# Attention feeding a softplus network: chunks of 512 tokens throughout, a larger token ring, and weight work moved between engines

## The chip, the cores and the metric

The kernel runs on one core of one Trainium2 chip. The metric is device time in microseconds (us) of one execution; lower is better. Five engines work side by side, each on its own queue in order: TensorE (PE in the profile, with its weight loads as PEld), VectorE (DVE), ScalarE (ACT), GpSimd (POOL) and SyncE (SP), which here only starts transfers. They wait for each other by semaphores.

## What is computed

```python
# q, k, v: (8, 8, 576, 64), q and k large, so that the softmax is sharp
scores = q @ k.transpose(0, 1, 3, 2) / sqrt(64)
local   = (rel >= 0) & (rel < 32)                  # heads 0..3, rel = row - column
strided = (rel >= 0) & (same position modulo 32)   # heads 4..7
attn = softmax(where(mask, scores, -1e9))
x = (attn @ v).transpose(0, 2, 1, 3).reshape(4608, 512)
h = x @ w_in                                       # 512 x 2048
g = max(h, 0) + log1p(exp(-abs(h)))                # softplus
out = g @ w_out                                    # 2048 x 512
```

The network's weights arrive as float64, 8 bytes each, and are turned into float32 on the chip. Because the products must be more exact than one pass of TensorE in its fast 32-bit format, every operand of the network is kept as a high part and a low part (value minus high part), and each product is made of three: high by high, high by low weight, low by high weight.

## The kernel before, in words

**Attention.** Work goes by pairs of heads: 8 batches of 4 pairs, n = 0 to 31. A pair's steps are: load queries (`load_q`), keys (`load_k`) and values (`load_v`); lay the queries out (`lay_out_q`, lines 252 and 254); the scores of nine chunks of 64 keys in two parts (`scores`, line 315); the softmax on VectorE and ScalarE (lines 334 to 405); transposing the probabilities, in the first batch on TensorE with copies back (`early_transposes`, `early_copy`, lines 430 to 451), later on VectorE (`prob_transposes`, line 415); the weighted sums (`weighted`, line 466); and writing the result as high part (ScalarE, line 491) and low part (VectorE, line 489) into the token buffers (`x_part`). These buffers hold 1152 tokens, two batches, as a ring.

**Weights.** Both matrices are cut into 16 tiles of 128 x 512, 32 in all. Each is rebuilt from the two 32-bit halves of its float64 values: magnitude (`w_abs`, ScalarE, line 516), shift (`w_shift`, VectorE, line 520), sign (`w_sign`, VectorE, line 526), the last three bits from the lower half (`w_last`, VectorE, line 532), then the high part (`w_high`, ScalarE, line 538) and the low part (`w_low`, VectorE or GpSimd, line 542).

**Network.** Tokens go through it in chunks: 512, 256, and then ten of 384. A step is one chunk by one of 16 slices of 128 hidden units: the hidden product (`hidden`, line 556, 12 matmuls as wide as the chunk, tile `ph`), the softplus (`log_part` on ScalarE, lines 568 to 573, `softplus` on VectorE, line 577), its high and low part (`g_high`, `g_low`, lines 585 to 592), and the output product two steps later (`output`, line 599, 3 matmuls of 512 columns for each 128 tokens, tile `py`, one accumulator bank for each 128 tokens). At a chunk's end the banks are copied out and stored (`result`, lines 610 and 612).

**Order.** The first stage, attention of batches 0 and 1, all weight work, chunk 0 and the beginning of chunk 1, is written out by hand as a list of names, `FIRST`. A letter names the step and the number its pair or tile: q, k, v loads; D query layout; S scores; X, Y, x, E, Z, r, R, M softmax; T and C or P transposes; V weighted sums; H and L high and low token parts; wi and wo weight loads; a, B, c, d, h, l (with i or o) the six weight steps; F hidden; A, Ae, Al, u softplus; Gh, Gl parts; O output; Q... the same for chunk 1; y results. `ON_POOL` and `ON_VECTOR` name those that run on another engine than usual. Each engine gets its operations in the order of this list.

After that, `Plan` (a list scheduler with costs and due times written in the kernel) orders steps and pairs. The pairs of batches 2 to 7 are put between steps by `BATCH_AT`: four steps apart, batches 2 and 3 in chunks 2 and 3, 4 and 5 in chunks 5 and 6, 6 and 7 in chunks 8 and 9. Where another pair follows four steps later, its scores and the weighted sums of the pair before are one visit of TensorE (`joint`); the first pair of each group of eight has its scores alone, the last its sums alone. Four hidden steps of chunk 1 (`AHEAD`) belong to the written list.

**Buffers.** Laid-out queries, keys, transposed probabilities and values have two buffers each; accumulator memory has two banks for `ph`, four for `py`, one each for scores (`ps`) and sums (`po`). From batch 2 on the second part of the scores uses the fourth `py` bank, which chunks of 384 leave free.

Of the kernel before, what the change touches and what calls it, by code (L numbers as in the profile page):

```python
# [11 lines left out]
BF16 = mybir.dt.bfloat16  # L12
U32 = mybir.dt.uint32
# [22 lines left out]
q0 mask D01 W k0 D00 q1 D10 S00 D11 X00 Y00 S01 X01 x01 k1 wo5 q2 E00 Z00 S11 X11 S10 E01 r0 q3 R0  # L36
M0 k2 ao5 T01 D21 D20 D30 Bo5 co5 Y11 C01 do5 T00 C00 X10 x10 S20 X20 D31 T02 wi5 ai5 Bi5 E11 Z11
E10 ci5 S21 X21 di5 v0 V00 H00 C02 Y20 E20 k3 r1 x21 wi11 R1 M1 S31 L00 wi1 X31 v1 S30 Z20 V01
ai11 Bi11 E21 H01 T10 C10 wi2 ci11 di11 r2 x31 R2 T11 T12 L01 C11 V10 v2 ai1 X30 M2 wi0 Y30 T21
C12 ho5 lo5 hi5 wi3 li5 hi11 li11 H10 L10 v3 E30 Z30 E31 C21 r3 R3 T20 k5 C20 V11 H11 T22 Bi1 L11  # L40
# [12 lines left out]
X70 x70 hi13 hi12 li12 Gh8 Gl8 ho8 lo8 V51 u9 Gh9 Gl9 F10 A10 Ae10 P6 F12 v6 ai15 Bi15 H51 L51 O8
li13 Al10 u10 V60 F13 ao10 Bo10 co10 ai14 ao11 Bo11 E70 do10 ho10 Bi14 ci14 O9 di14 v7 ci15 di15
Gh10 Gl10 A12 Ae12 lo10 Al12 u12 S71 hi15 H60 A13 hi14 L60 ao12 co11 V61 H61 do11 li14 O10 L61
li15 X71 x71 E71 Bo12 co12 Gh12 Gl12 r7 R7 ho11 lo11 Ae13 M7 Al13 wo13 ao13 u13 Gh13 F14 Bo13 do12
O11 q8 D8 co13 do13 ho12 lo12 Gl13 F15 O12 ho13 lo13 P7 V70 A14 Ae14 ao14 Bo14 co14 O13 do14 A15
Ae15 Al14 u14 ao15 Bo15 H70 L70 V71 ho14 Qa0 Gh14 Gl14 lo14 O14 k9 co15 H71 do15 ho15 L71 Q0 q9
Al15 u15 QA0 Gh15 lo15 Gl15 Qu0 Qh0 Q2 O15 y0 y1 Ql0 QA2 Q1 Qu2 Qh2 Ob15 y3 QO0 QA1 Qu1 Q3 D9 k8
Qh1 Ql1 Ql2 QA3 Qu3 Qh3 v9 v8 y2 Ql3 QO1  # L60
# [9 lines left out]
ON_SCALAR = """  # L70

# [47 lines left out]
def attention_softplus_ffn(  # L119
# [21 lines left out]
    RING = 2 * S  # L141

    CH = [512, 256] + [384] * ((NT - 768) // 384)
# [7 lines left out]
    v_pool = ctx.enter_context(tc.tile_pool(name="v", bufs=2))  # L151
# [11 lines left out]

    qT_early, kT_early = (
        {
            n: x_pool.tile([P, RING], F32, tag=f"x{part}{PAIRS[n]}", name=f"early_{part}{n}")
            for n in (2, 3)
        }
        for part in "hl"
# [30 lines left out]
    nc.vector.memset(pt[0], 0.0)  # L200
    nc.gpsimd.memset(pt[1], 0.0)
# [3 lines left out]
    vs, pss, sts, pos = ({} for _ in range(4))  # L205
# [57 lines left out]
    def load_v(n):  # L263
        b, pair = order[n]
        if n < NPAIR:

            t = room[n]
        else:
            t = v_pool.tile([P, 2 * NTILE * D], F32, tag="v_in", name=f"v_{b}_{pair}")
# [13 lines left out]
    for n in range(NPAIR):  # L283
        zeros(n)
# [632 lines left out]
```

## Time and profile before

| | |
|---|---|
| median of 3 runs | 926.68 us (926.28 to 927.91) |
| the profiled execution: time | 927.21 us |
| its span, first to last instruction | 925.4 us |
| its granted TensorE clock, mean | 0.995 |
| TensorE busy | 908.2 us, 98% |
| VectorE busy | 622.5 us, 67% |
| ScalarE busy | 483.1 us, 52% |
| GpSimd busy | 63.0 us, 7% |
| read from and written to HBM | 47.91 MB and 9.44 MB |

The profile is of one execution. A page has the engines' busy time, then the span in 40 slices (a digit is the busy share in tenths; PEclk is the share of the clock that TensorE was granted). Other views of the same trace are used below: *windows* give each engine's busy time in stretches of the span; *groups* put instructions of one line, engine and tile together, with their count, busy time, mean length in ns, and the idle time before them with what ended it; the *chain of waits* goes back from the last instruction, at each step to what released it, and lists pieces with start and length; the *timeline* lists instructions in order. Matmuls are pipelined: their recorded lengths overlap, so the cost of one is the distance to the next start and not its length.

### The profile page before, as it was taken

The page shows a single profiled execution, that of the slowest core. Times are in us where ns is not written, and L with a number is a line of the kernel's source. Part 1 is how long each engine was busy: PE and PEld are TensorE (multiplying, and loading weights), DVE is VectorE, ACT ScalarE, POOL GpSimd, SP SyncE. Part 2 cuts the span into 40 slices and gives each one's busy share as a digit, 9 for nine tenths or more (in the row PEclk, how much of TensorE's full clock was granted, in tenths as well). Part 3 has the DMA queues.
Part 4 walks back from the last instruction along what each step waited for, and adds up shares of the span by engine and source line. Part 5 has one row for each costly group of instructions (what it writes and reads, how often), then busy time and mean ns, then how long its engine had stood idle before and what let it go on. Part 6 is the DMA issues. An engine that isn't in the chain of part 4 may idle for free.

```text
span 925.4 us, 16092 instructions
## 1 busy us (share of the span) xinstructions
PE 908.2 (98%) x6276; PEld 799.5 (86%) x6276; DVE 622.5 (67%) x1438; ACT 483.1 (52%) x935; POOL 63.0 (7%) x96
## 2 busy tenths in 40 slices
PE   7898999999999999999999999999999999999998
PEld 5586778998898888988899988989988898999997
DVE  8998995488878853367788873338888785433332
ACT  7887875455555544335555445335555543333433
POOL 4433530000000000000000000000000000000000
PEclk9998999999999999999999999999999999999999
DMA  9962302021122110002222111002112200000000
GB/s 332 324 234 94 104 26 92 1 79 43 55 78 72 44 30 35 1 14 89 58 57 77 45 54 51 1 1 89 43 43 64 69 17 1 35 1 1 35 1 34
DMA packets 49947, 58.37 MB, mean 63 GB/s; under 512 B 3152, under 2 KB 35024, under 8 KB 49872
## 3 DMA queue, kind: packets, MB, share of 16 engines
q1 hardware_dynamic: 49872, 57.36, 19.2%
q8 instruction: 49, 0.80, 0.4%
q14 instruction: 26, 0.21, 0.1%
HBM read 47.91 MB, written 9.44 MB: 62 GB/s over the span
## 4 chain that ended last, share of the span: by engine, by line
PE 88%; DVE 7%; ACT 2%; issue 2%; DMA 1%; POOL 1%; SPq 0%; DVEq 0%; POOLq 0%
PE py L599 42%; PE ph L556 40%; PE po L466 3%; PE ps L315 2%; DVE pt L415 2%; PE py L315 1%; DVE a_i L526 1%; DVE a_i L532 1%; DVE u L577 1%; DVE a_i L520 1%; DMA raw_q<-in_qk_dram 1%; DVE a_o L526 0%; DMA prob<-in_qk_dram 0%; ACT prob L357 0%; DVE a_o L532 0%
## 5 line engine op out<-in xcount | busy, mean ns | idle before, releaser
L556 PE MATMUL ph<-x_h,w_i 128*128 128x384 f32 (+2 forms) x1536 | 392.3, 338 | 1.2 <-DVE u L577 1.2
L599 PE MATMUL py<-w_o,gh 128*128 128x512 f32 x1152 | 365.2, 398 | 0.0
L556 PEld LDWEIGHTS ph<-x_h,w_i 128*128 128x128 f32 x1536 | 279.9, 188 | 22.7 <-DVE u L577 2.0
L568 ACT ACTIVATE u<-ph 128x384 f32<-128x384 f32 (+2 forms) x192 | 94.3, 491 | 377.3 <-PE ph L556 373.7
L556 PE MATMUL ph<-x_l,w_i 128*128 128x384 f32 (+2 forms) x768 | 259.6, 338 | 0.0
L577 DVE SCALAR_TENSOR_TENSOR u<-ph,u 128x384 f32<-128x384 f32 (+2 forms) x192 | 106.8, 556 | 226.3 <-ACT u L573 224.8
L599 PEld LDWEIGHTS py<-w_o,gh 128*128 128x128 f32 x1152 | 212.8, 190 | 38.9 <-issue 0.2
L599 PE MATMUL py<-w_o,gl 128*128 128x512 f32 x576 | 228.8, 397 | 0.0
L556 PEld LDWEIGHTS ph<-x_l,w_i 128*128 128x128 f32 x768 | 144.3, 188 | 2.6
L415 DVE STREAM_TRANSPOSE pt<-prob 32x192 f32<-32x192 f32 x448 | 137.2, 314 | 6.4 <-POOL prob L405 0.3
L599 PEld LDWEIGHTS py<-w_o,gl 128*128 128x128 f32 x576 | 108.9, 189 | 25.1
L592 DVE TENSOR_TENSOR gl<-u,gh 128x384 fp32r<-128x384 f32 (+2 forms) x185 | 103.4, 559 | 15.5
L571 ACT ACTIVATE u<-u 128x384 f32<-128x384 f32 (+2 forms) x192 | 100.8, 525 | 5.9
L573 ACT ACTIVATE u<-u 128x384 f32<-128x384 f32 (+2 forms) x192 | 100.7, 525 | 5.9
L587 DVE CAST gh<-u 128x384 fp32r<-128x384 f32 (+2 forms) x183 | 65.2, 356 | 15.1 <-DVE u L577 0.5
L272 POOL MEMSET v<- 32x128 f32 x28 | 6.0, 216 | 591.2 <-PE po L466 591.2
L466 PE MATMUL po<-pt,v 128*64 128x96 f32 x672 | 34.1, 250 | 3.6 <-POOL v L272 3.2
L252 ACT COPY qT<-prob 64x576 f32<-64x576 f32 x28 | 35.5, 1268 | 1.5 <-DMA prob<-in_qk_dram 1.5
L254 ACT COPY qT<-prob 64x576 f32<-64x576 f32 x28 | 34.9, 1245 | 0.3
L491 ACT CAST x_h<-po 128x288 fp32r<-128x288 f32 x64 | 25.4, 399 | 17.9 <-PE po L466 13.4
L466 PEld LDWEIGHTS po<-pt,v 128*64 128x64 f32 x672 | 29.3, 139 | 5.8 <-POOL v L272 3.3
L489 DVE TENSOR_TENSOR x_l<-po,x_h 128x288 fp32r<-128x288 f32 x64 | 28.6, 448 | 6.0 <-ACT x_h L491 5.9
(81 smaller groups left out, 508.4 us busy)
## 6 DMA issues: line engine op xcount, KB each, us to landing
out_dram<-o SPq DMA_DIRECT2D x36, 256.0 KB, 2.3
v<-in_v_dram SPq DMA_DIRECT2D x28, 320.0 KB, 3.5
kT<-in_qk_dram SPq DMA_DIRECT2D x30, 288.0 KB, 3.0
ro<-in_moe_w_out_dram SPq DMA_DIRECT2D x16, 512.0 KB, 7.1
ri<-in_moe_w_in_dram SPq DMA_DIRECT2D x16, 512.0 KB, 7.2
prob<-in_qk_dram SPq DMA_DIRECT2D x28, 288.0 KB, 2.8
v<-in_v_dram SPq DMA_DIRECT2D x28, 48.0 KB, 2.8
room<-in_v_dram SPq DMA_DIRECT2D x4, 320.0 KB, 6.2
```

Source lines behind the costliest of these rows:

```text
L252: copy(to[rows, :, h], raw_q[rows])
L254: copy(to[rows, :, h].rearrange("p m l -> p l m"), raw_q[rows].rearrange("p m l -> p l m"),)
L415: nc.vector.transpose(pt[n % 2][32 * (i + c) : 32 * (i + c) + 32, h, a : a + hi - lo, 32 * i : 32 * i + 32,], src[:, lo:hi, 32 * c : 32 * ...
L466: nc.tensor.matmul(po[64 * h : 64 * h + 64, TILE * x : TILE * x + TILE], lhsT=vs[n][:, a, h, :], rhs=pt[n % 2][:, h, a, :], start=True, st ...
L556: nc.tensor.matmul(ph, lhsT=w32["i", f][:, half, cc * P : (cc + 1) * P], rhs=x_of(x, cc)[:, t0 : t0 + n], start=(i == 0), stop=(i == 3 * N ...
L568: nc.scalar.activation(us[c, f], phs[c, f], AF.Abs)
L571: nc.scalar.activation(u, u, AF.Exp, scale=-1.0)
L573: nc.scalar.activation(u, u, AF.Ln, bias=1.0)
L577: nc.vector.scalar_tensor_tensor(u, in0=phs.pop((c, f)), scalar=0.0, in1=u, op0=ALU.max, op1=ALU.add)
L587: nc.vector.tensor_copy(g, us[c, f])
L592: engine.tensor_tensor(g, us.pop((c, f)), ghs[c, f].bitcast(F32), op=ALU.subtract)
L599: nc.tensor.matmul(py[t], lhsT=g[:, sl], rhs=w32["o", f][:, half], start=(f == 0 and n == 0), stop=(f == NFC - 1 and n == 2),)
```

## The change

- All nine chunks have 512 tokens; the token ring grows from 1152 to 1536 and is written in two pieces where a batch crosses its end.
- Laid-out queries, transposed probabilities and values have one buffer instead of two; keys keep two. In the first batch all four pairs' queries and keys, and the transposed probabilities of pairs 1 and 3, lie in the token buffers before these are used.
- The second part of the scores shares the `po` bank with the sums of the pair before, since four `py` banks are now always in use.
- The last-bits step can run on GpSimd as a byte operation on the raw weights (29 of 32 tiles do); the sign step then keeps those bits and the separate `or` on VectorE goes. High parts (11 of 32) and one `Gh` run on GpSimd too. 21 instead of 11 low parts of weights and 6 instead of 1 normalizations (M) run on VectorE in the list.
- The zero rows in front of values and keys are written once, not for each pair; two zero fills of the transposed probabilities are gone.
- Batch 2 starts at the first planned step with a pair every three steps; from batch 3 on a pair comes every four steps, without gaps, so that all visits but the first and last are joint. `AHEAD` is 2.
- `FIRST`, `ON_POOL`, `ON_VECTOR` and `ON_SCALAR` are new lists.

The diff, cut to its core:

```diff
 ON_POOL = """
-x10 r1 x21 r3 x40 x50 x51 r5 x60 r6 x70 x71
+D01 x01 x10 D31 D30 di4 di0 x21 hi0 x31 di1 di2 do1 di3 hi3 ho1 hi2 do0 do5 ho0 Gh0 di5 hi5 do2
+do3 di8 di6 do4 x51 di7 di9 hi7 do6 x60 do7 do9 ho7 r6 do8 di10 hi12 di13 do11 do10 di15 do12 do13
+ho12 di14 do14 ho15
 """.split()
 ON_VECTOR = """
-D00 D10 M0 D20 C00 C11 C12 li5 C21 C30 li1 lo0 Gh0 Gl0 Gl1 li4 Gl2 lo2 Gh4 Gl4 li10 Gh6 Gl6 li8
-Gh7 lo9 Gl10 li14 Gh12 Gl12 lo11 Gh13 Gl14 lo14 Gh15 Gl15 y0
+D10 D20 M0 M1 M2 C21 M3 C31 lo1 li2 li11 li3 Gh1 Gl0 lo0 Gl1 li5 M4 Gl3 li8 lo4 li6 M5 li7 lo6 lo9
+Gh7 lo7 Gl7 lo8 li13 Gl10 lo11 lo10 Gl11 li15 li14 lo13 Gh15 Gh14 Gl15 Gl14 lo14
 """.split()
...
-    RING = 2 * S
-
-    CH = [512, 256] + [384] * ((NT - 768) // 384)
+    CH = [512] * (NT // 512)
+    RING = 3 * 512
...
-    pt = [const.tile([P, 2, NTILE, TILE], F32, name=f"pt_{i}") for i in range(2)]
-    qT = [const.tile([P, 2 * S], F32, name=f"qT_{i}") for i in range(2)]
+    pt = const.tile([P, 2, NTILE, TILE], F32, name="pt")
+    qT = const.tile([P, 2 * S], F32, name="qT")
     kT = [const.tile([P, PAD + S], F32, name=f"kT_{i}") for i in range(2)]
+    v_in = const.tile([P, 2 * NTILE * D], F32, name="v_in")
...
-            ps = py[3]
+            shared[n] = ps_o.tile([P, 512], F32, tag="po", name=f"po_{n}")
+            ps = shared[n][:, S // 2 :]
...
+        if joint:
+            if half == 0:
+                po = shared[n + 1]
+            else:
+                po = ps_h.tile([P, 512], F32, tag="ph", name=f"pv_{n}")
...
+    def w_last(w, f, engine):
...
+        if engine is nc.vector:
...
+        else:
+            by = raw[w, f][2]
+            engine.tensor_scalar(
+                by[:, :, 4], by[:, :, 3], 1 / 32, -31 / 64, op0=ALU.mult, op1=ALU.add
+            )
+            kept[w, f] = 0x80000007
...
     def w_sign(w, f):
         a = part[w, f]
         nc.vector.scalar_tensor_tensor(
-            a, in0=raw[w, f][1], scalar=0x80000000, in1=a, op0=ALU.bitwise_and, op1=ALU.bitwise_or
+            a,
+            in0=raw[w, f][1],
+            scalar=kept.get((w, f), 0x80000000),
...
-    def w_high(w, f):
+    def w_high(w, f, engine):
         w32[w, f] = w_pool.tile([P, 2, DM], F32R, tag=f"w{w}{f}", name=f"w_{w}_{f}")
-        nc.scalar.copy(w32[w, f][:, 0], part[w, f].bitcast(F32))
+        copy_on(engine, w32[w, f][:, 0], part[w, f].bitcast(F32))
...
-    AHEAD = 4
+    AHEAD = 2
...
-    BATCH_AT = {2: 2, 3: 3, 5: 4, 6: 5, 8: 6, 9: 7}
-    EVERY, EARLY = 4, 2
...
+    pair_at = {begin + 3 * i: 2 * NPAIR + i for i in range(NPAIR)}
+    for b in range(3, B):
+        for i in range(NPAIR):
+            pair_at[NFC * (b - 1) - 2 + 4 * i] = NPAIR * b + i
```

More of the change, by code (lines that the diff above doesn't have):

```diff
@@ L35 @@
 FIRST = """
[L36 to L40, printed above, removed]
@@ L53 @@
[L53 to L58, printed above, removed]
@@ L161, in attention_softplus_ffn @@
     nc.scalar.preload_act_table_set("natural_log_exp_and_others")
-    qT_early, kT_early = (
[L165 to L169, printed above, removed]
+    early = {
+        (part, pair): x_pool.tile([P, RING], F32, tag=f"x{part}{pair}", name=f"early_{part}{pair}")
+        for pair in PAIRS
+        for part in "hl"
+    }
+    qT_early, kT_early = (
+        [early[part, pair][:, :width] for pair in PAIRS]
+        for part, width in (("h", 2 * S), ("l", PAD + S))
     )
@@ L199, in attention_softplus_ffn @@
     nc.scalar.copy(ident, ident_b)
-    nc.vector.memset(pt[0], 0.0)
-    nc.gpsimd.memset(pt[1], 0.0)
     order = [(b, p) for b in range(B) for p in PAIRS]
-    vs, pss, sts, pos = ({} for _ in range(4))
+    vs, pss, sts, pos, shared = ({} for _ in range(5))
     taken = []
@@ L281, in load_v @@
         vs[n] = t.rearrange("p a (h d) -> p a h d", d=D)
-    for n in range(NPAIR):
+    for n in range(NPAIR + 1):
         zeros(n)
+    for t in kT:
+        nc.gpsimd.memset(t[:, :PAD], 0.0)
+    for t in room + [v_in]:
+        nc.gpsimd.memset(t[0:PAD, : 2 * D], 0.0)
     def mask_of(n, part):
@@ L476, in x_part @@
         m = S // 2
-        base = (b % 2) * S
         src = pos[n, half][:, :m]
-        if is_local(n):
-            cut = lambda t: t[:, base + half * m : base + half * m + m]
+        local = is_local(n)
+        if local:
+            first, each = b * S + half * m, 1
+            dst = lambda t, lo, hi: t[:, lo:hi]
+            cut = lambda lo, hi: src[:, lo:hi]
         else:
             nr = STRIDE // 2
+            first, each = b * S, STRIDE
             src = src.rearrange("p (r t) -> p t r", r=nr)
-            cut = lambda t: t[:, base : base + S].rearrange("p (t r) -> p t r", r=STRIDE)[
+            dst = lambda t, lo, hi: t[:, lo:hi].rearrange("p (t r) -> p t r", r=STRIDE)[
                 :, :, nr * half : nr * half + nr
             ]
-        if low:
-            high = x_of("h", pair).bitcast(F32)
-            nc.vector.tensor_tensor(cut(x_of("l", pair)), src, cut(high), op=ALU.subtract)
-        else:
-            nc.scalar.copy(cut(x_of("h", pair)), src)
+            cut = lambda lo, hi: src[:, lo // STRIDE : hi // STRIDE]
+        first %= RING
+        size = m if local else S
+        end = min(size, RING - first)
+        for lo, hi in ((0, end), (end, size)):
+            if lo == hi:
+                continue
+            at = (first + lo) % RING
+            place = lambda part: dst(x_of(part, pair), at, at + hi - lo)
+            if low:
+                high = dst(x_of("h", pair).bitcast(F32), at, at + hi - lo)
+                nc.vector.tensor_tensor(place("l"), cut(lo, hi), high, op=ALU.subtract)
+            else:
+                nc.scalar.copy(place("h"), cut(lo, hi))
     def load_weights(w, f):
@@ L629, in task, with of @@
         first[name] = lambda: fn(*args)
-    def either(name, usual, other):
-        return other if name in ON_POOL + ON_VECTOR + ON_SCALAR else usual
+    def of(name, usual):
+        for names, engine in ((ON_POOL, nc.gpsimd), (ON_VECTOR, nc.vector), (ON_SCALAR, nc.scalar)):
+            if name in names:
+                return engine
+        return usual
     first["mask"] = lambda: nc.sync.dma_start(mask_b, masks)
@@ L821, in attention_softplus_ffn @@
             after = [name]
-        made, z = made_by[n], when[i + EVERY] + (1.9 if i + EVERY in pair_at else 0.6)
-        if i + EVERY not in pair_at:
-            add(made, when[i + EVERY], "PE", 1.3, lambda n=n: sums_of(n), [f"P{n}", f"v{n}"])
+        made, z = f"S{n+1}", when[i_of[n + 1]] + 1.9 if n != last else 0
+        if n == last:
+            made, z = f"V{n}", when[i + 4] + 0.6
+            add(made, when[i + 4], "PE", 1.3, lambda n=n: sums_of(n), [f"P{n}", f"v{n}"])
         for half in range(2):
             z += 0.6
+            left = order[n][0] * S - RING
             after = [made] + [
@@ L830, in attention_softplus_ffn @@
                 for c in range(NCHUNK)
-                if START[c] < (order[n][0] - 1) * S and START[c] + CH[c] > (order[n][0] - 2) * S
+                if START[c] < left + S and START[c] + CH[c] > left
             ]
```

198 lines of the change are left out of this document (105 added, 93 removed).

## The prediction

> **What bounds the kernel now.** I read the page first: the engines' shares, then the forty slices (here TensorE's and the granted clock's).
>
> ```profile
> span 925.4 us, 16092 instructions
> PE 908.2 (98%) x6276; PEld 799.5 (86%) x6276; DVE 622.5 (67%) x1438; ACT 483.1 (52%) x935; POOL 63.0 (7%) x96
> PE   7898999999999999999999999999999999999998
> PEclk9998999999999999999999999999999999999999
> ```
>
> TensorE is busy for 98% of the span. What is missing lies in the first slices, one of which has a lower clock. The windows say how much, stage by stage, and what the other engines do there.
>
> ```profile
> core 0: us, PE busy (x) PEld busy (x) DVE busy (x) ACT busy (x) POOL busy (x), PEclk, DMA share, GB/s
> 0.00:20.00 20.00, 15.10 (x260) 9.79 (x260) 15.59 (x34) 15.13 (x39) 8.03 (x24) 1.00 0.96 326
> 20.00:40.00 20.00, 16.81 (x337) 12.24 (x337) 19.28 (x37) 17.02 (x39) 9.89 (x10) 1.00 0.90 313
> 40.00:60.00 20.00, 19.07 (x93) 15.06 (x92) 19.66 (x34) 17.43 (x42) 3.66 (x5) 1.00 1.00 363
> 60.00:80.00 20.00, 16.30 (x100) 12.56 (x99) 19.52 (x42) 18.12 (x45) 9.28 (x10) 0.85 0.38 136
> 80.00:100.00 20.00, 20.00 (x136) 16.01 (x135) 17.02 (x37) 15.18 (x34) 8.34 (x7) 0.98 0.20 61
> 100.00:140.00 40.00, 39.58 (x246) 31.05 (x244) 38.55 (x87) 30.27 (x71) 17.70 (x17) 1.00 0.15 46
> 140.00:920.00 780.00, 779.75 (x5110) 701.86 (x5107) 492.18 (x1172) 368.83 (x669) 6.17 (x25) 1.00 0.13 41
> ```
>
> So there are two stages. From 140 us on TensorE idles 0.25 us in 780: only fewer or shorter matmuls shorten this stage, and VectorE (492 of 780) has room. Before 140 us TensorE idles 4.90 us in the first window and 3.19 + 0.93 + 3.70 + 0.42 = 8.24 us in the others, while VectorE is 96 to 98% busy in four of the six: there VectorE's queue (attention of the first two batches and the rebuilding of the weights) sets the pace.
>
> A busy share can't say how fast matmuls follow each other, because they overlap. The chain of waits can: it is an unbroken row of TensorE work, so that the distance between two starts is the cost. First the stage of 384 tokens, with a visit of attention in the middle.
>
> ```profile
> 231.26 2.11 PE ph L556 x12
> 233.37 2.09 PE py L599 x9
> 235.46 2.11 PE ph L556 x12
> 237.57 0.85 PE ps L315 x24
> 238.42 0.35 PE py L315 x12
> 238.77 0.99 PE po L466 x24
> 239.76 2.28 PE py L599 x9
> 242.04 2.10 PE ph L556 x12
> ```
>
> A plain step (hidden x12, output x9) takes 235.46 - 231.26 = 4.20 us, one with a visit 242.04 - 235.46 = 6.58, so a visit costs 2.38 us, of which 0.85 + 0.35 + 0.99 = 2.19 are its own matmuls and 0.19 its edges. Now two steps of 512 tokens (both x12) and one of the single chunk of 256; in an unbroken row a piece's length is the distance to the next start.
>
> ```profile
> 49.77 2.73 PE ph L556 x12
> 52.50 2.80 PE py L599 x12
> ```
>
> ```profile
> 124.73 2.77 PE ph L556 x12
> 127.50 2.79 PE py L599 x12
> ```
>
> ```profile
> 160.02 1.43 PE ph L556 x12
> 161.45 1.39 PE py L599 x6
> ```
>
> A step of 512 takes 2.73 + 2.80 = 5.53 or 2.77 + 2.79 = 5.56 us, a step of 256 takes 2.82. For 512 tokens that is 5.53 to 5.56 at width 512, 4.20 x 4/3 = 5.60 at 384, and 5.64 at 256.
>
> **The change, part by part, against the profiled execution's own 927.21 us (span 925.4 and 1.8 around it).**
>
> *Width.* Chunk 0 has 512 tokens already. The 3840 tokens in chunks of 384 become 7.5 chunks of 512, which is 7.5 x 16 = 120 steps; the 256 become half a chunk, 8 steps. I take 5.55 for the new step: 120 x (5.60 - 5.55) = 6.0 us, and 8 x (5.64 - 5.55) = 0.7. Sum -6.7. With 5.53 it is 120 x 0.07 + 8 x 0.11 = 9.3, with 5.56 it is 120 x 0.04 + 8 x 0.08 = 5.4. The gain is all in the hidden product; the output product has the same matmuls as before, at 512 in both. The Trainium skill, "TensorE: Matmul & The Clock Gate", section "Back-to-back issue gap", gives an isolated warm matmul N / 2.4 + 2.5 ns: only the 2.5 ns don't shrink with N. By it a step would save 16 - 12 = 4 of these, 10 ns, and all 120 steps 1.2 us (an estimate from that page); the trace's 40 to 70 ns a step differ from it.
>
> *Joint visits.* Attention of batches 2 to 7 is 24 pairs. Before, they run in three groups of eight, so that six visits do only scores or only sums; after, the pairs form one unbroken row, with two such visits. Four edges of about 0.19 go: -0.6 to -0.8 us, taken as 0.6.
>
> *The front.* The byte operation replaces VectorE's third rebuilding step (line 532) on 29 of 32 weight tiles, and 10 of the low parts (line 542) and 5 normalizations (line 405) go from GpSimd to VectorE; 11 high parts (line 538) go from ScalarE to GpSimd.
>
> ```profile
> L532 DVE SCALAR_TENSOR_TENSOR a_i<-ri,a_i 128x512 uint32<-128x512 uint32 x16 | 12.9, 814 | 0.3
> L532 DVE SCALAR_TENSOR_TENSOR a_o<-ro,a_o 128x512 uint32<-128x512 uint32 x15 | 11.3, 752 | 0.3
> L542 DVE TENSOR_TENSOR w_i<-a_i,w_i 128x512 fp32r<-128x512 f32 x6 | 4.2, 701 | 0.0
> L405 DVE TENSOR_TENSOR prob<-prob,st 128x576 f32<-128x576 f32 x1 | 0.8, 757 | 0.0
> L538 ACT CAST w_o<-a_o 128x512 fp32r<-128x512 f32 x15 | 9.2, 618 | 1.6 <-DVE a_o L532 1.6
> L542 POOL TENSOR_TENSOR w_i<-a_i,w_i 128x512 fp32r<-128x512 f32 x10 | 14.1, 1415 | 13.9 <-ACT w_i L538 13.9
> L405 POOL TENSOR_TENSOR prob<-prob,st 128x576 f32<-128x576 f32 x7 | 8.7, 1238 | 17.7 <-DMA ri<-in_moe_w_in_dram 7.3 <-DVE st L401 6.5 <-ACT u L571 2.2
> L201 POOL MEMSET pt<- 128x1152 f32 x1 | 1.1, 1062 | 0.0
> ```
>
> VectorE: 14 x 0.814 + 15 x 0.752 = 22.7 us go, 10 x 0.701 + 5 x 0.757 = 10.8 come, net -11.9; the six windows hold 15.59 + 19.28 + 19.66 + 19.52 + 17.02 + 38.55 = 129.62, 93% of 140 us, and 117.7 is 84%. ScalarE loses 11 x 0.618 = 6.8 us. No row shows a byte operation on GpSimd. From below it is its memset, 1062 / 1152 x 512 = 0.47 us; from above an operation of two full operands, 1.42; bytes could also be handled far slower than either, which is a rival below. I take 0.9, nearer the memset, since it reads one narrow operand, and the same for a high part. GpSimd, with 8.03 + 9.89 + 3.66 + 9.28 + 8.34 + 17.70 = 56.90 us in the six windows, then has 56.90 - 10 x 1.42 - 5 x 1.24 + 40 x 0.9 = 72.5 us of work in 140: not a bound. The sign step on VectorE now waits for GpSimd's byte operation; what is queued behind it are maxima, softplus sums and transposes, so a late byte would hold all of VectorE. Smaller moves (three half layouts of queries to GpSimd, three early copies to ScalarE, some guards to VectorE) are left out of the sum.
>
> What can come back is the idle time after the first window, 8.24 us, and what a slow clock took.
>
> ```profile
> 68.89 5.07 issue
> ...
> 76.03 5.20 PE py L599 x12
> ```
>
> Here the chain has 5.07 us in which it waits for nothing that the profile shows: backlogs of VectorE and ScalarE, which are both over 90% busy in that window. The output product that follows takes 5.20 us instead of 2.79, and the granted clock of that window is 0.85. That is 2.41 more, so 10.65 in all. The first window's 4.90 us stay: queries and keys have to land. I take 8.0, three quarters, since the chain of scores, exponentials and transposes up to the first hidden product is latency as much as load. From the other side: nothing, if VectorE fills up again; at most 10.65.
>
> *Waits that are added, at nothing.* A single buffer of transposed probabilities: its writer runs after the scores that share a TensorE visit with the last reader, so the wait is there already. Single queries: the layout on ScalarE waits for the scores of the pair before; two steps, 11 us, cover it. Single values: the load is queued on SP behind the sums that read the old ones, ahead of the next queries and keys, with at least three steps, 16.6 us, until its use. Batch 2 is now done with a pair every three steps of 5.55 and a visit, 19.0 us; before, a pair had four of 4.20 and a visit, 19.2, and there TensorE idled nowhere. The transition from the written order, with two steps ahead instead of four, is shorter: I add 0.5 us for all this, with 0 to 4 as bounds.
>
> Sum: 927.21 - 6.7 - 0.6 - 8.0 + 0.5 = 912.4 for a profiled execution. The profiled one is 0.5 over the median of 926.68, so 912.
>
> **The rivals.**
>
> *The shared access takes the front's gain back.* Two rows of the front, of VectorE and of GpSimd:
>
> ```profile
> 116.89 1.78 DVE L526 SCALAR_TENSOR_TENSOR a_i<-ri,a_i 128x512 uint32<-128x512 uint32 x1
> ```
>
> ```profile
> 116.30 1.83 POOL L542 TENSOR_TENSOR w_o<-a_o,w_o 128x512 fp32r<-128x512 f32 x1 [2.64 <-ACT w_o L538]
> ```
>
> VectorE's operation took 1.78 us, 1.0 more than the mean of its kind and shape at line 532 (0.75 to 0.81), and it began 0.59 us into an operation of GpSimd that itself took 0.4 longer than its mean. After the change GpSimd has 40 more operations that read SBUF and 15 fewer. If half of the 25 extra ones hold VectorE up by 1.0, that is 12.5 us, more than the 11.9 that go, and the front stays as long as it is: 912 + 8 = 920. For it: that row; against it: the new operations are shorter, if 0.9 holds. The Trainium skill, "SBUF — State Buffer", section "Who interferes with whom", has this as an exclusive lock on a port pair, taken by VectorE operations with two SBUF inputs or in a two-port mode; the trace's 1.78 beside 0.81 agrees.
>
> *Width brings next to nothing.* If the steady hidden product costs what the output product costs at the same width, 2.79, a step is 5.58 and the width brings 120 x 0.02 + 8 x 0.06 = 2.9: 912 + 3.8 = 916. The Trainium skill's gap rule, cited above, points the same way.
>
> *Slower: byte operations too slow on GpSimd.* All 29 have to be done in some 120 us of the first 140, from the first weights to chunk 0's last step, beside 72.5 - 29 x 0.9 = 46.4 us of other work on that queue. Past (120 - 46.4) / 29 = 2.5 us each they, and the sign steps that wait for them, set the front's end; past 3.0 us (another 14.7 / 29) the kernel is slower than before. At 4 us: 912 + 29 x 1.5 = 955. Nothing in the trace shows a GpSimd operation of 512 elements over 1.42 us on the mean, which speaks against it.
>
> *The single buffers cost after all.* If each of 23 visits waits 0.6 us, 13.8 us are lost: 926, no change. Against it is the idle 0.25 us in 780 at the same tightness.
>
> **How the numbers follow.** Forecast (both gains) 0.58; shared access 0.19; width without gain 0.10; slow bytes 0.07; single buffers or a front that gains nothing beside a narrow width gain, so no change, 0.06. The range runs from 926.7 - 9.3 - 0.8 - 10.65 = 905.9, rounded outward to 905, to the first rival's 920, and one more for what that front might add: 921. A measurement of this kernel tells 0.2%, about 1.9 us, from no change. Faster 0.87, same 0.06, slower 0.07.
>
> **What would show it.** Right: 12 hidden matmuls from start to start near 2.76 us in every chunk, two-kind steps of 5.55; VectorE busy clearly under 129 us in the first 140; no lower clock after the start; TensorE idle by less than 5 us between 20 and 140 us. Wrong: hidden groups of 2.79 or more; many VectorE operations of 1.6 to 1.8 us beside byte operations; GpSimd near full in the front; TensorE waits after 140 us at the visits or at the first pair of batch 2.

## The result and the profile after

The changed kernel took 932.25 us (median of 6 runs, 931.70 to 935.55) beside 926.72 for the kernel before (6 runs, 926.28 to 927.91): a ratio of 1.0065, 95% interval 1.0049 to 1.008. It is 5.5 us slower, and the forecast was 912. The profiled execution took 932.19 us, with a span of 929.7.

The page of the changed kernel, with the span, the engines' shares, TensorE's slices and the granted clock:

```profile
span 929.7 us, 14475 instructions
PE 902.6 (97%) x5700; PEld 725.8 (78%) x5700; DVE 609.5 (66%) x1291; ACT 445.7 (48%) x792; POOL 94.0 (10%) x97
PE   7889889999999999999999999999999999999998
PEclk8999999999999999999999999999999999999999
```

TensorE is busy 5.6 us less than before (908.2) and the span is 4.3 us longer, so it waits more, and the gaps lie in the first slices again. The windows of the changed kernel, in the columns that the prediction used:

```profile
0.00:20.00 20.00, 13.29 (x190) 8.15 (x193) 10.13 (x21) 10.86 (x29) 11.45 (x31) 0.88 0.96 322
20.00:40.00 20.00, 17.60 (x381) 12.94 (x375) 18.76 (x33) 14.58 (x38) 15.03 (x14) 0.95 0.56 192
40.00:60.00 20.00, 17.48 (x106) 13.42 (x105) 19.30 (x32) 16.75 (x42) 10.16 (x10) 1.00 1.05 395
60.00:80.00 20.00, 17.26 (x122) 13.41 (x121) 19.53 (x39) 15.65 (x41) 14.62 (x12) 1.00 0.36 113
80.00:100.00 20.00, 19.11 (x123) 15.17 (x122) 19.73 (x40) 17.68 (x40) 12.33 (x10) 1.00 0.51 174
100.00:140.00 40.00, 32.85 (x195) 24.66 (x194) 38.33 (x69) 24.44 (x60) 25.22 (x20) 1.00 0.10 31
140.00:920.00 780.00, 779.39 (x4578) 633.87 (x4577) 481.18 (x1058) 344.52 (x546) 5.22 (x4) 1.00 0.14 41
```

The last row, the steady stage, is as full as before. Between 20 and 140 us TensorE idles 2.40 + 2.52 + 2.74 + 0.89 + 7.15 = 15.70 us, where it was 8.24, and VectorE is as full there as it was (115.65 us of 120, before 114.03). With the first window it is busy for 10.13 + 18.76 + 19.30 + 19.53 + 19.73 + 38.33 = 125.78 us of 140, where 117.7 was forecast.

Two stages thus went two ways. First the steady one, in the chain of waits of the changed kernel, with a visit of attention at 511 us:

```profile
497.51 2.76 PE ph L607 x12
500.27 2.80 PE py L647 x12
503.06 2.76 PE ph L607 x12
...
508.62 2.75 PE ph L607 x12
511.37 0.85 PE ps L332 x24
512.22 0.35 PE po L332 x12
512.57 0.50 PE po L484 x12
513.06 0.49 PE pv L484 x12
513.56 2.98 PE py L647 x12
516.54 2.77 PE ph L607 x12
```

A step takes 503.06 - 497.51 = 5.55 us, and one with a visit 516.54 - 508.62 = 7.92, so the visit still costs 2.37.

To split the whole, I took each matmul's start from the trace and the start of the next, and counted as TensorE's waits what lies between them beyond the usual distance of its kind in an unbroken row. From the first matmul to the end of the last, the work came to 897.4 us before and 888.4 after, 9.0 less. The waits up to 200 us were 23.7 before and 35.5 after, 11.8 more; from there on they are -0.6 and +0.5, 1.1 more. Together that is 3.9 of the 4.3 us by which the span grew. Nearly all of the loss is therefore in the front. There, the groups of the changed kernel in the first 160 us:

```profile
L571 POOL TENSOR_SCALAR ro<-ro 128x512 uint8<-128x512 uint8 x15 | 22.4, 1494 | 11.2 <-ACT a_o L548 10.5
L571 POOL TENSOR_SCALAR ri<-ri 128x512 uint8<-128x512 uint8 x14 | 20.7, 1478 | 4.2 <-issue 2.7 <-ACT a_i L548 0.6
L552 DVE TENSOR_SCALAR a_o<-a_o 128x512 uint32<-128x512 uint32 x16 | 15.5, 979 | 0.1
L552 DVE TENSOR_SCALAR a_i<-a_i 128x512 uint32<-128x512 uint32 x16 | 13.8, 869 | 0.1
L593 DVE TENSOR_TENSOR w_i<-a_i,w_i 128x512 fp32r<-128x512 f32 x10 | 9.4, 939 | 0.3 <-ACT w_i L256 0.3
L422 DVE TENSOR_TENSOR prob<-prob,st 128x576 f32<-128x576 f32 x6 | 7.4, 1234 | 0.1
```

and the shift step (line 552 here, 520 there) in the kernel before:

```profile
L520 DVE TENSOR_SCALAR a_i<-a_i 128x512 uint32<-128x512 uint32 x16 | 8.8, 554 | 0.3 <-ACT a_i L516 0.3
L520 DVE TENSOR_SCALAR a_o<-a_o 128x512 uint32<-128x512 uint32 x16 | 7.9, 493 | 0.0
```

A byte operation takes 1.49 us instead of the 0.9 that was taken, and the shift, whose code did not change, rose from 554 and 493 ns to 869 and 979. A mean hides what happened to the single ones; the timeline shows it. GpSimd's queue in the changed kernel:

```profile
79.37 1.77 POOL L571 TENSOR_SCALAR ri<-ri 128x512 uint8<-128x512 uint8 x1 [0.40 <-ACT a_i L548]
82.51 1.54 POOL L571 TENSOR_SCALAR ro<-ro 128x512 uint8<-128x512 uint8 x1 [0.30 <-ACT a_o L548]
```

and VectorE's at the same place:

```profile
79.83 0.45 DVE L520 TENSOR_TENSOR x_l<-pv,x_h 128x288 fp32r<-128x288 f32 x1
80.20 1.21 DVE L578 SCALAR_TENSOR_TENSOR a_i<-ri,a_i 128x512 uint32<-128x512 uint32 x1
81.33 0.41 DVE L552 TENSOR_SCALAR a_i<-a_i 128x512 uint32<-128x512 uint32 x1
82.75 1.58 DVE L552 TENSOR_SCALAR a_o<-a_o 128x512 uint32<-128x512 uint32 x1
```

The first byte operation ends at 79.37 + 1.77 = 81.14. The shift at 81.33, after it, takes 0.41 us. The shift at 82.75 meets the second, which ends at 82.51 + 1.54 = 84.05, and itself ends at 84.33, 0.28 later, as if it had stood still until GpSimd was done. The step at 80.20 did the same; the one at 79.83, which reads PSUM, took its usual time in the middle of a byte operation. The other shifts bear this out: all 15 shifts that are lengthened in the changed kernel end 0.28 to 0.29 us after an operation of GpSimd ends, although they begin anywhere from 0.12 to 0.59 us after its start.

Counting each VectorE operation of the first 160 us that took over 0.2 us more than is usual for its kind and shape, with the excess summed, I call it the lengthening: 13 operations and 10.9 us before, 35 and 31.5 us after, 16.0 of these in 15 shifts. Of the 29 byte operations 23 lay beside such a lengthening, 21.5 us in all.

### The profile page after: what moved, and what is told of

It reads as the page before. It is cut to its first block, busy times and chain, and to the rows that moved or that the text cites. A ratio compares the mean times of both kernels' runs of the same rounds, so it can differ in the third digit from the quotient of the medians.

```text
span 929.7 us, 14475 instructions
## 1 busy us (share of the span) xinstructions
PE 902.6 (97%) x5700; PEld 725.8 (78%) x5700; DVE 609.5 (66%) x1291; ACT 445.7 (48%) x792; POOL 94.0 (10%) x97
## 4 chain that ended last, share of the span: by engine, by line
PE 85%; DVE 11%; DMA 1%; issue 1%; POOL 1%; ACT 1%; SPq 0%; DVEq 0%; POOLq 0%; ACTq 0%
PE py L647 40%; PE ph L607 38%; PE ps L332 2%; DVE pt L432 2%; PE pv L484 2%; DVE a_o L552 1%; PE po L484 1%; DVE a_o L578 1%; PE po L332 1%; DVE a_i L552 1%; DMA ri<-in_moe_w_in_dram 1%; DVE u L628 1%; DVE w_i L593 1%; DVE a_i L578 1%; DVE gl L640 1%
## 5 line engine op out<-in xcount | busy, mean ns | idle before, releaser
L607 PE MATMUL ph<-x_h,w_i 128*128 128x512 f32 x1152 | 359.2, 392 | 8.8 <-DVE u L628 6.8
L619 ACT ACTIVATE u<-ph 128x512 f32<-128x512 f32 x144 | 86.2, 598 | 410.2 <-PE ph L607 409.7
L607 PEld LDWEIGHTS ph<-x_h,w_i 128*128 128x128 f32 x1152 | 215.6, 188 | 59.2 <-DVE u L628 7.6
L607 PE MATMUL ph<-x_l,w_i 128*128 128x512 f32 x576 | 225.9, 392 | 0.0
L628 DVE SCALAR_TENSOR_TENSOR u<-ph,u 128x512 f32<-128x512 f32 x144 | 99.0, 688 | 178.9 <-ACT u L624 177.0
L607 PEld LDWEIGHTS ph<-x_l,w_i 128*128 128x128 f32 x576 | 108.1, 188 | 25.2 <-DVE x_l L520 0.2
L640 DVE TENSOR_TENSOR gl<-u,gh 128x512 fp32r<-128x512 f32 x136 | 95.7, 705 | 11.1 <-DVE gh L256 0.5
L622 ACT ACTIVATE u<-u 128x512 f32<-128x512 f32 x144 | 91.0, 632 | 4.5
L624 ACT ACTIVATE u<-u 128x512 f32<-128x512 f32 x144 | 90.9, 631 | 4.5
L256 DVE CAST gh<-u 128x512 fp32r<-128x512 f32 x132 | 56.8, 430 | 10.7 <-PE py L647 0.5
L332 PEld LDWEIGHTS ps<-kT,qT 128*64 128x64 f32 x720 | 23.6, 137 | 11.2 <-issue 10.5
L332 PE MATMUL ps<-kT,qT 128*64 128x64 f32 x720 | 28.0, 226 | 0.0
L484 PE MATMUL pv<-pt,v_in 128*64 128x96 f32 x396 | 22.5, 248 | 1.4 <-DVE pt L432 1.3
L571 POOL TENSOR_SCALAR ro<-ro 128x512 uint8<-128x512 uint8 x15 | 22.4, 1494 | 11.2 <-ACT a_o L548 10.5
```

What stands on the lines that cost most here:

```text
L256: (engine.copy if engine is nc.scalar else engine.tensor_copy)(dst, src)
L332: nc.tensor.matmul(ps[64 * place : 64 * place + 64, 64 * (x - lo) : 64 * (x - lo) + 64], lhsT=blocks_of(n)[:, c // 32].rearrange("p h l -> ...
L484: nc.tensor.matmul(po[64 * h : 64 * h + 64, TILE * x : TILE * x + TILE], lhsT=vs[n][:, a, h, :], rhs=pt_of(n, a)[:, h, a % 2], start=True, ...
L607: nc.tensor.matmul(ph, lhsT=w32["i", f][:, half, cc * P : (cc + 1) * P], rhs=x_of(x, cc)[:, t0 : t0 + n], start=(i == 0), stop=(i == 3 * N ...
L619: nc.scalar.activation(us[c, f], phs[c, f], AF.Abs)
L622: nc.scalar.activation(u, u, AF.Exp, scale=-1.0)
```

## The experiments

Theory A: the front's loss is the byte operations on GpSimd, which take long and hold up VectorE's own operations. Rivals: the start (a layout of queries behind GpSimd's zeroing; the first scores begin at 8.67 us, before at 6.23), transfers that start late behind single buffers, and the rest of the new lists and order. The times stand beside the kernel before on the same chip, 926.8 to 927.1 us; a ratio is against it. "Waits" are TensorE's up to 200 us, as above.

### Byte operations away

The 29 last-bits steps that run as byte operations are left out.

```diff
-            engine.tensor_scalar(by[:, :, 4], by[:, :, 3], 1 / 32, -31 / 64, ...)
-            kept[w, f] = 0x80000007
+            kept[w, f] = 0x80000000
```

> The changed kernel without the 29 byte operations on GpSimd: the last three bits of 29 weight tiles are left out, so the output is less exact; the sign step keeps its old mask, nothing else moves. Theory A (shared access): VectorE operations that meet a byte operation are stretched, by 21.5 us in the changed kernel's trace, and VectorE is the bound of the front; without them VectorE's 134 us of the first 150 fall to about 112 and the front ends 10 to 20 us sooner: 912 to 922 us. Theory B (the new lists: a later start, because the first scores wait for a query layout on GpSimd, and transfers stuck behind waits in SyncE's queue): the front stays as long, 929 to 933 us.

Measured: 913.26 us, ratio 0.9847 [0.9834, 0.9861], so 19.0 us less than the changed kernel. Waits 16.7, lengthening 9.1 us. As theory A has it, 19 us hang on the byte operations. This kernel is also what the prediction reckoned with, a last-bits step that costs VectorE nothing (here it costs GpSimd nothing either). Its first 140 us in one window:

```profile
0.00:140.00 140.00, 132.24 (x1195) 101.42 (x1196) 118.80 (x257) 109.47 (x262) 49.95 (x68) 1.00 0.54 186
```

VectorE is busy for 118.80 us, where 117.7 was forecast, and the time is 1.3 us from the forecast's 912.

### The step back on VectorE, and on ScalarE

```diff
-ON_POOL = """ ... di4 di0 ... do1 ... do14 ... """
+ON_POOL = """ the same without the d names """
```

> The changed kernel with all last-bits steps back on VectorE (29 x 0.69 = 20 us more work there), GpSimd keeps the rest. Theory A: the 20 us that come are what the stretching took (21.5), so next to nothing changes: 929 to 935 us. Theory B, by which the byte operation costs VectorE nothing: the front grows by most of 20 us: 945 to 952 us.

Measured: 928.24 us, 1.0015 [1.0006, 1.0024], just under theory A's 929. Waits 31.6, lengthening 11.1 us. Done on VectorE the step costs 928.2 - 913.3 = 15.0 us, done on GpSimd 19.0: GpSimd is the worse place by 4.0 us, although it relieves VectorE of an operation each time. In VectorE's own time the two are about even, 31.5 - 11.1 = 20.4 us of lengthening beside 29 x 0.69 = 20.0 us of operations; from where the 4.0 us come was not traced.

```diff
-            engine.tensor_scalar(by[:, :, 4], by[:, :, 3], 1 / 32, -31 / 64, ...)
+            nc.scalar.activation(by[:, :, 4], by[:, :, 3], AF.Copy, bias=-31 / 64, scale=1 / 32)
```

> The changed kernel with the same byte operation done by ScalarE in place of GpSimd. Theory A: ScalarE doesn't share an access with VectorE; VectorE loses the 21.5 us of stretching, ScalarE gains 29 x 0.6 = 17 us beside its 106 of the first 150, which it can take: 915 to 924 us, faster than both kernels. Theory B: no faster than the changed kernel, 930 to 940 us, since ScalarE has more to do and the lists are the same.

Measured: 938.37 us, 1.0119 [1.0105, 1.0133], a miss. Lengthening is down to 6.6 us, but the groups of this kernel show another price than expected:

```profile
L571 ACT ACTIVATE ro<-ro 128x512 uint8<-128x512 uint8 x15 | 20.6, 1370 | 0.1
L571 ACT ACTIVATE ri<-ri 128x512 uint8<-128x512 uint8 x14 | 19.0, 1378 | 0.1
L576 DVE SCALAR_TENSOR_TENSOR a_i<-ri,a_i 128x512 uint32<-128x512 uint32 x16 | 11.0, 693 | 12.0 <-ACT ri L571 12.0
L576 DVE SCALAR_TENSOR_TENSOR a_o<-ro,a_o 128x512 uint32<-128x512 uint32 x16 | 11.0, 687 | 7.8 <-ACT ro L571 7.8
```

1.37 us each on ScalarE, and VectorE's sign steps waited 12.0 + 7.8 us for it (last columns). The long time of the byte operation belongs to its bytes, not to GpSimd; the lengthening of VectorE belongs to GpSimd.

### The start, and the transfers

Three half layouts of queries went to ScalarE; in another kernel four loads of weights stood ahead of pair 4's queries, and one ahead of pair 6's values.

```diff
-ON_POOL = """ D01 x01 x10 D31 D30 ... """
+ON_POOL = """ x01 x10 ... """
```

> The changed kernel with the three half layouts of queries (D01, D30, D31) on ScalarE in place of GpSimd. The first scores start at 8.7 us in the changed kernel and at 6.2 before. Theory B: the start moves 2 us or more ahead and with it the whole full VectorE queue: 927 to 930 us. Theory A alone: the bound is VectorE's total work, but it starts with the scores too, so a gain of up to 2.5 us fits it as well; no gain (931 to 933) would say that the start is not part of the loss.

Measured: 931.82 us, 1.0045 [1.0032, 1.0057], waits 36.1. This edit did not do what it was made for. On ScalarE the layouts were done hardly sooner, and the first scores began at 8.47 us instead of 8.67:

```profile
8.47 0.91 PE L332 MATMUL py<-early_l,early_h 128*64 128x64 f32 x12 [2.62 <-ACT early_h L256]
```

What the start at 8.67 us instead of 6.23 costs is therefore not tested. It is no part of the 19 us, since the run without byte operations began its scores at 8.65.

```diff
-FIRST = """ ... q4 ... wo6 wi11 ... wo5 ... wi13 ... v6 ... wo14 ... """
+FIRST = """ ... wo6 wi11 wo5 wi13 q4 ... wo14 v6 ... """
```

> The changed kernel with four weight loads put ahead of the queries of pair 4, and the load of the last output tile ahead of the values of pair 6, so that they don't stand in SyncE's queue behind waits of 11.8 us (at 20 to 32 us of the span) and of 15 and 8 us (at 102 to 126 us). Theory A: VectorE is full all that time with other work, so at most 2 us are gained: 930 to 933. Theory B: 924 to 928.

Measured: 932.04 us, 1.0067 [1.0051, 1.0082], waits 35.6. The transfers' share between 20 and 40 us rose from 0.56 to 0.85, as meant, and nothing followed: these transfers don't set the front's end.

### Writing alone, and the form of the shift

Two byte writes stand in place of each byte operation, which take no input; the last three bits are left out.

```diff
-            engine.tensor_scalar(by[:, :, 4], by[:, :, 3], 1 / 32, -31 / 64, ...)
+            engine.memset(by[:, :, 4], 0)
+            engine.memset(by[:, :, 4], 0)
```

> The changed kernel with each byte operation replaced by two memsets of the same 512 bytes on GpSimd: an operation that writes with the same stride and reads nothing; the last three bits are left out of the output. Theory A1 (what stretches VectorE is that GpSimd holds the access while it runs, reading or not): stretching stays in proportion to the memsets' length, and the time lies between the kernel without byte operations (913.3) and the changed one (932), near 922 if two memsets are as long as one byte operation. Theory A2 (only reading stretches): 913 to 915 us.

Measured: 944.75 us, 1.0199 [1.0186, 1.0212], a miss for both theories. The two writes together take longer (2.7 us) than the one operation that they stand for, against what was meant, so the time can't be compared straight. Lengthening 44.3 us, 36.5 of it beside these writes; per us of GpSimd's time that is 36.5 / 78 = 0.47, and beside byte operations 21.5 / 43 = 0.50. Reading by GpSimd is not needed for it. The groups of this kernel:

```profile
L552 DVE TENSOR_SCALAR a_i<-a_i 128x512 uint32<-128x512 uint32 x16 | 22.0, 1379 | 0.1
L552 DVE TENSOR_SCALAR a_o<-a_o 128x512 uint32<-128x512 uint32 x16 | 21.6, 1360 | 0.6 <-ACT a_o L548 0.5
L571 POOL MEMSET ro<- 128x512 uint8 x15 | 19.6, 1306 | 6.4 <-ACT a_o L548 6.3
L572 POOL MEMSET ro<- 128x512 uint8 x15 | 20.7, 1377 | 0.9
```

Nearly all of it sits in the shift: 24 of the 28 that ran beside GpSimd, 30.4 us, and all 24 end 0.28 to 0.29 us after a GpSimd operation ends; of the two-input sign steps it was 1 of 16. So the next pair gave the shift a second input, in this kernel and in the changed one.

```diff
-        nc.vector.tensor_scalar(
-            a, a, 3, 0x7FFFFFFF, op0=ALU.logical_shift_left, op1=ALU.bitwise_and
-        )
+        nc.vector.scalar_tensor_tensor(
+            a, in0=a, scalar=3, in1=low31.to_broadcast([P, DM]),
+            op0=ALU.logical_shift_left, op1=ALU.bitwise_and
+        )
```

> The kernel with two byte writes in place of each byte operation (its last three bits left out as there), and in it the shift step in another form: the mask 0x7FFFFFFF comes from a column in SBUF, so the shift has a second input. An operation with a second input takes 0.68 us (the sign step) against 0.42: 32 x 0.26 = 8.3 us more VectorE work. In the parent 24 of 28 shifts beside GpSimd were lengthened, by 30.4 us in all, while the two-input sign step was lengthened in 1 of 16. Theory L (it is the shift's quick one-input form that can't run beside GpSimd's writes): fewer than 5 of the shifts are lengthened by more than 0.2 us, the lengthening of VectorE falls from 36.5 to under 12 us, and the time falls in spite of the longer form, from 944.8 to 925 to 937. Rival S (whatever stands at that place in the order is lengthened, since it is there that GpSimd is released): 20 us or more stay, and the time is 945 to 955.

> The changed kernel with the two-input form of the shift; nothing is left out of the computation. The byte operation reads SBUF as well as writing it, and beside it 5 of 11 of the two-input sign steps were lengthened in the changed kernel, 10 of 17 in the old order. Theory L: the shifts are lengthened somewhat less (16.0 us now; 10 of 9.9 us overlap by the sign's 4.3 us gives about 21.7 x 0.43 = 9.4 us), a gain of 6.6 us against 8.3 us of longer form: within 4 us of the changed kernel's 932.3. Rival S: no less lengthening, 8 us slower: 938 or more. If the reading does no harm either: 16 us less, 924 or less.

Measured: 930.28 us, 1.0033 [1.002, 1.0047], and 936.45 us, 1.0112 [1.0094, 1.0129]. The shift with a second input beside writes alone:

```profile
L557 DVE SCALAR_TENSOR_TENSOR a_o<-a_o,low 128x512 uint32<-128x512 uint32 x16 | 11.6, 736 | 0.3 <-ACT a_o L553 0.2
L557 DVE SCALAR_TENSOR_TENSOR a_i<-a_i,low 128x512 uint32<-128x512 uint32 x16 | 10.8, 682 | 0.1
```

and beside byte operations:

```profile
L557 DVE SCALAR_TENSOR_TENSOR a_o<-a_o,low 128x512 uint32<-128x512 uint32 x16 | 16.7, 1056 | 0.1
L557 DVE SCALAR_TENSOR_TENSOR a_i<-a_i,low 128x512 uint32<-128x512 uint32 x16 | 16.4, 1030 | 0.1
```

Beside writes, 2 of 28 shifts are lengthened, by 0.8 us in all (30.4 before), the whole lengthening falls from 44.3 to 14.4 us, and the kernel is 14.5 us faster although each shift takes 0.68 instead of 0.42 us. Theory L holds, rival S is out: it is the quick one-input form that doesn't run beside GpSimd's writes. In the kernel with byte operations, which also read, 14 of the 21 shifts beside GpSimd are lengthened, by 11.6 us (9.4 expected, 16.0 in the quick form), so that the form's 8 us are not paid for: 4.2 us slower than the changed kernel, just past the 4 us that were expected. The form doesn't mend the loss.

### Moving other work

Low parts and normalizations were put back on GpSimd, the last-bits step on VectorE; then high parts went to GpSimd, with eleven late byte operations on ScalarE and the other last-bits steps on VectorE.

```diff
-ON_VECTOR = """ ... M1 M2 ... M3 ... lo1 li2 ... M4 ... lo13 ... """
+ON_VECTOR = """ the same without M1 to M5 and 14 low parts """
```

> The changed kernel with the last-bits steps on VectorE and, besides, 14 low parts of weights and 5 normalizations given back to GpSimd: the division of work nearly as before, with the new order, widths and buffers. VectorE loses 14 x 0.60 + 5 x 0.79 = 12.4 us against the run with the last-bits steps on VectorE (928.2); 19 more reading operations on GpSimd at 0.3 to 0.5 us of stretching each give 6 to 9 us back. Theory A: 921 to 925 us. Theory B (the new order itself costs, whatever the engines): 927 to 932.

Measured: 934.33 us, 1.0081 [1.0068, 1.0094], a miss, above what either theory expected. Waits 39.4, lengthening 27.2 us. Low parts on GpSimd, which in the kernel before lie beside a lengthening in 7 of 21 cases (5.9 us), do so here in 20 of 25 (15.1 us). How much an operation on GpSimd costs VectorE depends on what the order puts beside it.

```diff
-ON_POOL = """ ... di4 di0 ... """
+ON_POOL = """ no d names; all 32 h names """
-ON_SCALAR = """ y3 """
+ON_SCALAR = """ y3 di10 di12 di13 di15 di14 do10 do11 do12 do13 do14 do15 """
```

> A version that should beat both kernels: from the changed one, all 32 high parts on GpSimd (its copies hardly stretched VectorE: 0.4 to 1.1 us in all for 12), 11 late byte operations on ScalarE (1.37 us each there, 15 us, against 21 x 0.52 = 11 us of high parts that leave it), the other 21 last-bits steps on VectorE. Against the run without byte operations (913.3) VectorE has 18 x 0.61 = 11 us more: theory A gives 918 to 924 us. If copies on GpSimd stretch VectorE like byte operations (0.74 each), 20 more of them cost 15 us and the time is 928 to 935.

Measured: 932.24 us, 1.0059 [1.0047, 1.0071]. That misses the 918 to 924 that were aimed at and lies in the 928 to 935 of the other case, but not by that case's reason alone. Lengthening 16.9 us, waits 35.7: high parts on GpSimd took 0.8 us, and 12 of its 33 casts lengthened something on VectorE, by 4.4 us and not 15.

### The new structure with the old lists

All else of the change (chunks, ring, single buffers, visits), with the order and the engine lists of the kernel before; then the byte operations alone added to that; then the new order with the old lists.

```diff
 # first
-FIRST, ON_POOL, ON_VECTOR, ON_SCALAR of the changed kernel
+those of the kernel before, less 14 names that have no place in it; v5 behind V41, v7 behind V61
 # second, beside that
+ON_POOL: the 29 d names, each ahead of its c in FIRST
 # third
 FIRST of the changed kernel
+ON_POOL, ON_VECTOR, ON_SCALAR of the kernel before
```

> The new structure (chunks of 512, ring of 1536, single buffers, joint visits) with the order by hand and the engine lists of the kernel before, less the fourteen names that two steps ahead have no place for; the loads of pairs 5 and 7's values stand behind the values' last use. Nothing is left out of the computation. Theory A (the steady stage brought about what the prediction's first two terms said, and the front's new lists lost it): 926.8 - 7.3 = 919.5, and up to 3 us less since the TensorE work measured fell by 10; range 915 to 922; about 24 us of TensorE waits before 150 us, as before. Rival C (single buffers or the wide ring cost the front what it lost): no faster than 924, with waits of TensorE over 30 us in the first 150 us.

> The kernel of the run before this one with one thing more: the same 29 last-bits steps as byte operations on GpSimd, each just before its sign step. Nothing is left out of the computation. VectorE is rid of 29 x 0.78 = 22.7 us and GpSimd gets 43 us. Theory A1 (half of a byte operation's time comes back as lengthened VectorE operations, whatever the order): 21.5 us come back, VectorE's sum to 150 us stays within 3 us of the run before, and the time within -3 to +5 of it. Rival A2 (in the old order the byte operations fall beside other VectorE work and lengthen less, as the low parts did: 7 of 21 against 20 of 25): under 12 us come back and it is 5 us or more faster than the run before.

> The changed kernel with its new order, but with the engine lists of the kernel before (no byte operation, 15 fewer low parts on VectorE, the normalizations M1 to M3 and M4, M5 on GpSimd). Nothing is left out of the computation. If the byte operations and the moved engines are the whole loss: as the run with the old order and old lists, 915 to 922. If the new order is itself a part of the loss (it was made for VectorE's low parts and keeps GpSimd's low parts beside shifts): 930 or more, as with the 14 low parts put back (934.3).

Measured: 920.35 us, 0.9931 [0.9917, 0.9945]; 926.42 us, 0.9996 [0.9987, 1.0005]; 942.14 us, 1.0172 [1.0155, 1.0189]. Waits 22.5, 32.4 and 46.5; lengthening 10.3, 26.8 and 19.2 us. Two windows of the first, in the places where the changed kernel lost most:

```profile
60.00:80.00 20.00, 19.40 (x123) 15.07 (x122) 19.52 (x42) 18.13 (x45) 9.34 (x9) 1.00 0.13 45
100.00:140.00 40.00, 38.71 (x239) 30.27 (x234) 37.58 (x84) 30.37 (x66) 17.15 (x15) 1.00 0.17 54
```

TensorE idles 0.60 and 1.29 us there instead of 2.74 and 7.15, and VectorE is about as full (19.52 and 37.58 us, in the changed kernel 19.53 and 38.33): it gets more done in the same time. This version beats both kernels. The single buffers and the ring cost the front nothing that shows (rival C is out).

The second is 6.1 us slower than the first, just past the -3 to +5 of theory A1, and rival A2 (5 us faster) is out. The lengthening rose by 16.5 us, and these rows of it show a second cost:

```profile
L577 DVE SCALAR_TENSOR_TENSOR a_o<-ro,a_o 128x512 uint32<-128x512 uint32 x16 | 15.1, 952 | 3.0 <-POOL ro L570 2.2
L577 DVE SCALAR_TENSOR_TENSOR a_i<-ri,a_i 128x512 uint32<-128x512 uint32 x16 | 14.2, 890 | 5.8 <-POOL ri L570 5.1
```

The sign steps waited 2.2 + 5.1 us for byte operations; in the changed kernel, which puts the byte operations earlier, they waited for none. VectorE's sum to 150 us fell by 6.4 us, more than the 3 expected, but no time was won by it: its last weight step ends 9.7 us later (148.3 us beside 138.6), with 10.5 us more idle time before it, of which these waits are 7.3.

The third says that the new order belongs with its own lists: with the old ones it is 9.9 us slower still. What in the order makes it so was not taken apart.

## Why the prediction was wrong, point by point

**Width and visits: right.** The step is 5.55 us as taken, the hidden groups 2.75 to 2.77. The prediction's sum without its front term is 912.4 + 8.0 = 920.4 for a profiled execution, 919.9 for a median; the new structure with the old front measured 920.35. That they agree within 0.5 us is in part luck: in the changed kernel TensorE's work fell by 9.0 us, where the two terms had 7.3, and other small losses took the difference back. The rival "width brings next to nothing" is out: 5.55, not 5.58. So is "the single buffers cost after all": from 140 to 920 us the steady stage stands as full as before. The 0.5 us taken for added waits stands beside 1.1 us found after 200 us.

**The front: wrong, and the step that failed is the term of -8.0.** It came out as 932.25 - 920.35 = +11.9 us. Its sum put at nothing what a byte operation on GpSimd takes from VectorE. In the run without byte operations, where that holds, the term is 913.26 - 920.35 = -7.1 us and VectorE's 118.80 us are near the 117.7 forecast; with them 19.0 us came on top. The loss against the old front can also be split by the place of the step. Two parts of that are told apart. The last-bits step on GpSimd instead of VectorE costs 4.0 us in the new order (932.25 against 928.24) and 6.1 in the old one. The new order and lists without byte operations cost 928.24 - 920.35 = 7.9 us; they put low parts and normalizations on VectorE and begin the first scores at 8.67 us, where the version with the old lists begins them at 6.32. Giving most of those operations back to GpSimd made it 6.1 us slower still (934.33 against 928.24); otherwise the experiments don't split the 7.9, and this part of the cause stays open.

Three inputs of the term failed. "I take 0.9" for a byte operation was 1.49, past the upper bound of 1.42 that stood beside it; the bound came from operations on whole words, and the bytes lie 8 apart. "VectorE: net -11.9" counted operations at their mean durations in the kernel before and left the lengthening as it was: the lengthening grew by 31.5 - 10.9 = 20.6 us, more than the 11.9 that went. And "GpSimd 72.5 us of work in 140: not a bound" asked only whether GpSimd has time, not what its time takes from VectorE.

**"The shared access takes the front's gain back" was the mechanism, under-priced.** The rival had half of 25 extra operations at 1.0 us, 12.5 us, and ended where the front stays as it was (920). The runs have 23 of 29 byte operations beside a lengthening, 21.5 us. It let the loss stop at zero; nothing in its reasons did, since with 20.6 us of lengthening against 11.9 the balance was already on the other side. The row of 1.78 us that the prediction quoted pointed that way: with 1.0 us for each of 29 byte operations the sum would have been 920.4 - 11.9 + 29 = 937.5, slower than before. The Trainium skill, "SBUF — State Buffer", section "Who interferes with whom", has VectorE operations in a two-port mode blocked by any GpSimd operation, those with two SBUF inputs only by one that reads SBUF, and those with at most one SBUF input outside these modes never. The runs agree on all three: the quick shift 24 of 28 beside writes; the two-input shift 2 of 28 beside writes and 14 of 21 beside GpSimd in the kernel with byte operations; transposes and operations with one input in PSUM, 0 of 72 in the changed kernel. That the quick shift runs in such a mode is inferred from its being held up; no row names a mode. The prediction used the rule for the sign step and missed the shift, which has one input but ran in the quick form.

**"Slower: byte operations too slow on GpSimd"** gave the right sign by another way. It put the point at 2.5 us each. At 1.49 GpSimd was busy 88.81 of the first 140 us (the six windows), and no sign step waited for it: its queue doesn't bind here.

**Signs.** Of what was named for a wrong forecast, the long VectorE operations beside byte operations came. Of what was named for a right one, the hidden groups and the steps came; VectorE's 125.8 us are hardly "clearly under 129", the first two windows have a lower clock (0.88 and 0.95), and TensorE idled 15.7 us between 20 and 140 us, not "less than 5".

## What to carry to other kernels

Before work goes to GpSimd, list what VectorE will run beside it. In these runs one-input operations on SBUF in their quick form, and two-input ones if GpSimd read, mostly stood still until GpSimd was done, so that with a full queue VectorE paid about half of GpSimd's time on the moved operations (0.47 to 0.50); work that reads PSUM ran beside it free. By this a move pays only if it takes more off VectorE than that half: here 0.75 to 0.81 us went and half of 1.49 came back, so it hardly could. Where one change holds a sure gain and a doubtful one, run the sure part alone: here it was worth 6.7 us (920.35 beside 927.08). And an experiment's own trace shows whether its edit moved what it was meant to move: the one for the start moved it by 0.2 us of 2.4.

## What the runs showed of the hardware that was not expected

An operation on 512 bytes that lie 8 apart took 1.48 to 1.49 us on GpSimd and 1.37 to 1.38 on ScalarE, and a write of such bytes alone 1.27 to 1.38 on GpSimd, where a write of 1152 whole words took 1.06: the engine and the arithmetic make little difference. Whether the price lies in the one-byte type or in the distance of 8 bytes was not tried. A quick VectorE operation of 0.41 us took 1.58 beside one of these: it ended 0.28 us after that one's end, as did all the lengthened shifts, so that it waited for the end and was not merely slowed. Giving it a second input, which makes it 0.26 us longer by itself, made the kernel with byte writes 14.5 us faster.
